# Chunk bounds in four groups of 192 queries in place of three of 256, with a new order of the work

## The chip, the cores and the metric

The kernel runs on one core of one Trainium2 chip. The metric is the time of one execution in microseconds on the device; the median of several runs is compared. One further execution was taken with the hardware profiler; all rows shown in this document come from such profiled executions.

An engine runs its own list of instructions in the order in which they were written. PE is the matmul engine (PEld its weight loads), DVE, ACT and POOL are the three element-wise engines, and SP issues DMAs; ACT and POOL issue some DMAs too.

## The reference

`q`, `k`, `v` have the shape (4, 8, 768, 64): 4 batches, 8 heads, 768 positions, 64 values each. The 768 keys are cut into 24 chunks of 32.

```python
k_min, k_max = min and max of each chunk of keys, value by value
ub = np.sum(np.maximum(q * k_min, q * k_max), axis=-1)      # an upper bound, query x chunk
ub = np.where(causal, ub, -1e9)
top_chunks = np.argsort(ub, axis=-1)[..., -6:]              # 6 best chunks of each query
scores = scale * q @ k^T, kept where the chunk is selected and the key isn't later
attn = exp(scores - max) / sum;  x = attn @ v               # 3072 tokens x 512
xn = x / rms(x) * rms_g
out = (silu(xn @ w_gate) * (xn @ w_val)) @ w_out            # 512 -> 1536 -> 512
```

## The kernel before

**The order.** The kernel first records all work as steps (`add`, line 251): each has a name, the engines that can do it, a cost, steps that it waits for, and buffers that it opens and uses. `Order.run` (line 98) then plays through time with these costs. Whenever an engine is free it takes, of the steps that are ready and whose buffers are free, the one with the lowest rank; the ranks are the numbers of `RANK` (by kind of step) and `TIMES` (by pair, half and so on). Loads also wait for a modelled DMA queue (`load=`, bytes). The instructions are emitted in the order found, so the ranks decide at build time what each engine does after what, and for steps with two engines also which does them. On the chip nothing is rearranged.

**The work.** Heads are taken in 16 pairs (four batches of four pairs). For each pair:

- `prep` loads the natural `k` and `q` (`load`, line 473; SP issues, for pair 0 half of them on ACT's queue), turns them on PE (`pk`, `pq`, line 498) into tiles with the 64 values of two heads on 128 partitions, and copies these out of PSUM (`kt`, `qt`, through `evict`, line 294 on ACT, 298 on DVE or POOL). DVE makes the chunk minima and maxima (lines 526, 524) and relu(q) (`rt`, line 568); a small subtraction gives max-min (line 542). POOL casts `kt` and `qt` to bf16 into `ke` and `qs` (for pair 0 ACT can too).
- `bounds` (line 580): ub = k_min.q + (k_max-k_min).relu(q) as fp32 matmuls of 64 rows x 32 columns. The array works as small tiles: 2 heads (row halves) x `G`=3 query groups of 256 (column quarters, so one quarter stays empty), twice (q, then relu(q)). `ub_out` copies two banks of 96x256 to SBUF, and `up_turn` (line 606) turns them back in 4 fp32 transposes, so that queries are on partitions.
- `causal` (line 616) adds the causal mask `cmf`, `top` (12 MAX8, line 631) finds the sixth best, `pick` (lines 639, 644) writes a 0/1 selection into `selq`.
- `sel_turn` (line 652) turns the selection back in 6 bf16 transposes (`st`), and `sel_out` (line 662) copies it in two instructions of 64x768 into the lower or upper half of `qs`, beside the bf16 queries. The rows of `ke` beside the keys hold the chunk pattern `e_all`, so that one score matmul does q.k and masks the chunks that aren't selected.
- `scores` (line 695): per head 6 groups of up to 4 blocks of 128x128 (in the fourth pair 2+4, first for the first half of the queries): `sc` matmuls (line 720), exp on ACT (`pt`, line 737), `av` matmuls (line 756), division (`xb`, line 772). A score matmul needs all copies of `sel_out` of its pair.

When the four pairs of a batch are done (the first half of its queries, then the second), `norm` makes the RMS norm (line 784 on) and `ffn` (line 864) the gated layer of this half: 12 times `gp` (line 884), tanh (`sg`, line 891), `tg` (line 897), `vp` (line 905), `hh` (line 913), and then `po` (line 925) with its copy `osb` and the store. The FFN of one batch and the attention of the next are interleaved by the ranks. 48 matmuls on zeros (`busy`, line 341) with the very highest rank fill PE where it has nothing else at the start; when they are used up, PE just waits.

Buffers: 3 sets of `ke`/`qs` (a pair takes the set of the pair three before it, once that one's scores have read it), 8 PSUM banks in all, with at most 3 or 4 for each use.

Of the kernel before, what the change touches and what calls it, by code (L numbers as in the profile page):

```python
# [27 lines left out]
        av=-54.4, dif=153.56, eps=344.72, exp=240.32, kC=97.58, kE=-137.82, kT=-251.02,  # L28
        kload=-3.44, kmn=111.29, kmx=140.51, max=-119.32, qC=-50.04, qE=82.16, qT=78.53,
        qload=-6.31, relu=104.93, root=78.28, sc=-65.68, sel=-319.81, selC=97.58, selT=30.75,  # L30
        sq=-238.56, tp=-62.89, tpE=19.78, ub=-202.6, ubE=-209.78, ubm=-332.23, up=-63.52,
        vload=-104.93, xb=103.6, xs=136.36,
    ),
    dict(
        av=-215.29, dif=107.84, eps=-215.03, exp=7.63, gate=-8.03, hh=-205.95, kC=167.33,
        kE=72.49, kT=-66.96, kload=51.54, kmn=-276.29, kmx=192.91, mask=-58.77, max=54.84,
        out=129.36, po=13.13, poE=7.91, qC=306.28, qE=72.26, qT=40.02, qload=32.65, relu=60.21,
        root=-87.97, sc=-65.32, sel=94.37, selC=311.72, selT=-46.08, sq=135.68, tanh=225.22,
        tg=3.41, ub=56.8, ubE=-99.19, ubm=110.82, up=42.39, val=-2.21, vload=16.42, xT=6.57,
        xb=49.3, xs=44.15,  # L40
# [161 lines left out]
def kernel(  # L202
# [26 lines left out]
    G = 3  # L229
# [83 lines left out]
    SELQ = [const.tile([P, NT, 2, D], BF16, name=f"selq{i}") for i in range(SLOTS["selq"])]  # L313
    VX = [const.tile([P, 2 * NT, D + 1], BF16, name=f"vx{i}") for i in range(SLOTS["vext"])]
    e_all = const.tile([D, S], BF16, name="e_all")
    cmf = const.tile([P, NT, 2, NCH], FP32, name="cmf")
# [27 lines left out]
    for i in range(BUSY):  # L344
# [34 lines left out]
    for i in range(NB):  # L379
        if i == 0:  # L380
            c_ke[i] = add("ke0", "", {"DVE": 1.05, "ACT": 1.4}, {"ke0": 1.0}, lambda e: (
                evict(e, KE[0][0][D:2 * D, :], e_all[:]),
                evict(e, KE[0][1][0:D, :], e_all[:])), [c_e])
        else:
            c_ke[i] = add("ke", "SP", 1.0, {"ke": 1.0}, lambda e, i=i: (
                nc.sync.dma_start(out=KE[i][0][D:2 * D, :], in_=e_all[:]),
                nc.sync.dma_start(out=KE[i][1][0:D, :], in_=e_all[:])), [c_e], load=200000)

    def make_cmf(n):
        if n == 0:  # L390
            nc.gpsimd.memset(cmf[:], 0.0)
        for g4 in (2 * n, 2 * n + 1):
            nc.gpsimd.affine_select(
                out=cmf[32 * g4:32 * (g4 + 1)], in_=cmf[32 * g4:32 * (g4 + 1)],
                compare_op=ALU.is_ge, fill=-BIGC,
                base=g4, pattern=[[4, NT], [0, 2], [-1, NCH]], channel_multiplier=0,
            )

    c_cm = add("cmf", "POOL", 1.5, -70, lambda e: make_cmf(0), [c_e])
    c_cm = add("cmf", "POOL", 1.1, -69, lambda e: make_cmf(1), [c_cm])  # L400

    def make_tri(e):
# [11 lines left out]
        load=200000)  # L414
# [14 lines left out]
    for part in range(2):  # L429
        a = add("wg", "POOL", 0.8, {f"w{part}": 1.0},  # L430
                lambda e, part=part: load_w(part, wg, moe_w_gate), load=1200000)
        b_ = add("wv", "POOL", 0.8, {f"w{part}": 1.0, "w": 1.0},
                 lambda e, part=part: load_w(part, wv, moe_w_val), load=1200000)
        c_w.append((a, b_))
    c_wo = [add("wo", "POOL", 0.8, {f"w{2 + part}": 1.0}, lambda e, part=part: load_wo(part),
                load=1200000) for part in range(2)]
# [15 lines left out]
    def load_v(c, lr):  # L452
# [7 lines left out]
        c.vload = add("v", "POOL", 1.08, rank(lr, b, "vload"), go, c_vx, opens=[c.v], load=393216)  # L460

    def prep(c, i0, nb, at, lr):
# [7 lines left out]
        for w, src in (("k", k), ("q", q)):  # L470
# [12 lines left out]
            if p == 0:  # L483
                ld = [add(w + "load", "SP", 0.55, -200 + 2 * (w == "q") + r0 / 3,
                          lambda e, load=load, r0=r0: load(e, r0=r0, rn=3), opens=[nat[w]],
                          load=3 * P * 512) for r0 in range(0, nb, 3)]
            else:
                ld = [add(w + "load", "SP", 1.1, rank(lr, b, w + "load"), load, opens=[nat[w]],
                          load=n * 512)] * 2
# [86 lines left out]
        nj = nq // P  # L576
# [411 lines left out]
```

## Time and profile before

| | us |
|---|---|
| median of 3 runs | 328.93 (328.64 to 329.02) |
| the profiled execution | 328.01 |
| its span (first to last instruction) | 326.3 |
| PE busy in the span | 314.2 (96%) |
| DVE busy | 237.8 (73%) |
| ACT busy | 201.3 (62%) |
| POOL busy | 117.4 (36%) |

In the rows below "busy, mean ns of one" stands behind a count x; a row of the chain or of the timeline begins with its start and its length in us. The time of a run is some 1.7 us above the span of its trace.

### The profile page before, as it was taken

The page shows a single profiled execution, that of the slowest core. Times are in us where ns is not written, and L with a number is a line of the kernel's source. Part 1 is how long each engine was busy: PE and PEld are TensorE (multiplying, and loading weights), DVE is VectorE, ACT ScalarE, POOL GpSimd, SP SyncE. Part 2 cuts the span into 40 slices and gives each one's busy share as a digit, 9 for nine tenths or more (in the row PEclk, how much of TensorE's full clock was granted, in tenths as well). Part 3 has the DMA queues.
Part 4 walks back from the last instruction along what each step waited for, and adds up shares of the span by engine and source line. Part 5 has one row for each costly group of instructions (what it writes and reads, how often), then busy time and mean ns, then how long its engine had stood idle before and what let it go on. Part 6 is the DMA issues. An engine that isn't in the chain of part 4 may idle for free.

```text
span 326.3 us, 7875 instructions
## 1 busy us (share of the span) xinstructions
PE 314.2 (96%) x2953; PEld 200.1 (61%) x2972; DVE 237.8 (73%) x652; ACT 201.3 (62%) x440; POOL 117.4 (36%) x176
## 2 busy tenths in 40 slices
PE   5899998999999999999999999999999999999995
PEld 2568766666776655666586776655567645666442
DVE  3578988999997589867289989587885684788200
ACT  4349999944797872564595987834399924342121
POOL 8449763644287730016062374830023120000000
PEclk9799999999999999999999999999999999999999
DMA  9999999379908998503233034510000034000123
GB/s 174 231 216 193 200 214 208 57 148 163 126 5 78 160 221 174 145 19 26 96 85 25 2 27 41 101 45 3 32 2 2 3 104 121 3 0 2 64 77 116
DMA packets 92501, 30.25 MB, mean 93 GB/s; under 512 B 85424, under 2 KB 89264, under 8 KB 92464
## 3 DMA queue, kind: packets, MB, share of 16 engines
q1 hardware_dynamic: 62352, 21.50, 29.6%
q0 software_dynamic: 28512, 7.87, 24.3%
q10 hardware_dynamic: 1600, 0.39, 0.6%
q8 instruction: 23, 0.38, 0.5%
q14 instruction: 14, 0.11, 0.1%
HBM read 28.57 MB, written 6.29 MB: 107 GB/s over the span
## 4 chain that ended last, share of the span: by engine, by line
PE 86%; ACT 5%; issue 2%; DMA 2%; DVE 2%; POOL 2%; POOLq 0%; ACTq 0%
PE vp L905 18%; PE gp L884 18%; PE po L925 18%; PE sc L720 9%; PE av L756 6%; PE ub L586 5%; PE busy L341 4%; PE pk L498 3%; PE pq L498 3%; DMA vx<-in_v_dram 2%; PE up L610 2%; ACT pt L737 1%; PE st L655 1%; ACT junk L799 1%; ACT qs L294 1%
## 5 line engine op out<-in xcount | busy, mean ns | idle before, releaser
L737 ACT ACTIVATE pt<-sc 128x512 bf16<-128x512 f32 (+3 forms) x192 | 88.4, 598 | 2.5 <-PE sc L720 2.1
L891 ACT ACTIVATE sg<-gp 128x384 bf16<-128x384 f32 x96 | 47.8, 506 | 49.0 <-PE gp L884 46.6
L905 PE MATMUL vp<-xT,wv 128*128 128x384 bf16 x384 | 75.3, 326 | 0.0
L884 PE MATMUL gp<-xT,wg 128*128 128x384 bf16 x384 | 74.7, 326 | 0.0
L897 DVE SCALAR_TENSOR_TENSOR tg<-sg,gp 128x384 bf16<-128x384 bf16 x96 | 52.0, 549 | 18.4 <-ACT sg L891 16.4
L925 PE MATMUL po<-wo,hh 128*128 128x512 bf16 x271 | 64.5, 379 | 0.9
L913 DVE TENSOR_TENSOR hh<-vp,tg 128x384 bf16<-128x384 f32 x96 | 52.3, 552 | 6.3 <-PE vp L905 4.9
L720 PE MATMUL sc<-qs,ke 128*128 128x128 bf16 (+5 forms) x419 | 53.0, 250 | 0.5 <-ACT qs L294 0.4
L884 PEld LDWEIGHTS <-wg 128*128 128x128 bf16 x384 | 36.5, 98 | 23.7 <-issue 0.4
L743 POOL TENSOR_SCALAR_AFFINE_SELECT pt<-pt 128x512 bf16<-128x512 bf16 (+1 forms) x48 | 24.9, 534 | 72.4 <-ACT pt L737 72.0
L905 PEld LDWEIGHTS <-wv 128*128 128x128 bf16 x384 | 36.5, 98 | 23.1 <-issue 0.8
L925 PEld LDWEIGHTS <-hh 128*128 128x128 bf16 x288 | 27.7, 98 | 29.0
L756 PE MATMUL av<-vx,pt 128*128 128x65 bf16 x672 | 35.1, 194 | 2.2 <-ACT pt L737 1.3
L756 PEld LDWEIGHTS <-pt 128*128 128x128 bf16 x672 | 30.0, 98 | 11.6 <-ACT pt L737 2.5
L720 PEld LDWEIGHTS <-ke 128*128 128x128 bf16 (+1 forms) x420 | 30.2, 97 | 10.2 <-issue 1.7
L296 ACT ACTIVATE osb<-po 128x512 f32<-128x512 f32 x22 | 13.3, 605 | 37.4 <-PE po L925 37.4
L298 POOL CAST qs<-qt 64x768 bf16<-64x768 f32 x31 | 28.0, 906 | 17.2 <-ACT qt L294 8.4
L298 POOL CAST ke<-kt 64x768 bf16<-64x768 f32 x31 | 25.6, 827 | 4.0 <-PE sc L720 2.0
L828 DVE SCALAR_TENSOR_TENSOR xs<-xb,ri,gains 128x512 bf16<-128x512 bf16 x24 | 18.0, 775 | 2.3 <-POOL ri L820 2.3
L772 DVE TENSOR_TENSOR xb<-av,rden 128x384 bf16<-128x384 f32 (+1 forms) x34 | 18.2, 534 | 1.2
L498 PE MATMUL pq<-ident_f,qnat 128*128 128x128 f32 x96 | 15.9, 285 | 3.2 <-issue 3.1
L631 DVE MAX8 m<-ubm 128x8 f32<-128x24 f32 x192 | 18.6, 167 | 0.1
(72 smaller groups left out, 331.4 us busy)
## 6 DMA issues: line engine op xcount, KB each, us to landing
out_dram<-osb SPq DMA_DIRECT2D x24, 256.0 KB, 2.1
qnat<-in_q_dram SPq DMA_DIRECT2D x30, 192.0 KB, 4.5
knat<-in_k_dram SPq DMA_DIRECT2D x30, 192.0 KB, 5.1
vx<-in_v_dram POOLq DMA_DIRECT2D x16, 192.0 KB, 5.7
wg<-in_moe_w_gate_dram POOLq DMA_DIRECT2D x2, 768.0 KB, 8.7
wv<-in_moe_w_val_dram POOLq DMA_DIRECT2D x2, 768.0 KB, 9.1
wo<-in_moe_w_out_dram POOLq DMA_DIRECT2D x2, 768.0 KB, 8.2
ke<-e_all SPq DMA_DIRECT2D x4, 96.0 KB, 4.8
```

The costliest lines, as they stand in the source:

```text
L298: engine[e].tensor_copy(out_, in_)
L498: nc.tensor.transpose(t[:, j * P:(j + 1) * P], nat[w].tile[:, j0 + j].rearrange("p h d -> p (h d)"), ident_f[:])
L720: nc.tensor.matmul(t[:, x:x + m, :].rearrange("p a b -> p (a b)"), ke[kk, kb * P:(kb + 1) * P], qs[kk, q0 * P:(q0 + m) * P], start=not tri ...
L737: nc.scalar.activation(out=t[:, 0:nn, :], in_=sc.tile[:, 0:nn, :], func=ACT.Exp, scale=SCALE)
L743: nc.gpsimd.affine_select(out=pt.tile[:, 0:nd, :], in_=pt.tile[:, 0:nd, :], compare_op=ALU.is_ge, fill=0.0, base=0, pattern=[[0, nd], [1, ...
L756: nc.tensor.matmul(av.tile[:, qi - i0, :], pt.tile[:, x, :], VX[c.v.slot][:, hl * NT + kb, :], start=(begin and m == 0), stop=(left[0] == ...
L884: nc.tensor.matmul(t[:], wg[:, g, hs], XT[b].tile[:, g, cols], start=(g == 0), stop=(g == NP - 1))
L891: nc.scalar.activation(out=t[:], in_=gp.tile[:], func=ACT.Tanh, scale=0.5)
L897: nc.vector.scalar_tensor_tensor(out=t[:], in0=sg.tile[:], scalar=1.0, in1=gp.tile[:], op0=ALU.add, op1=ALU.mult)
L905: nc.tensor.matmul(t[:], wv[:, g, hs], XT[b].tile[:, g, cols], start=(g == 0), stop=(g == NP - 1))
L913: nc.vector.tensor_tensor(out=t[:], in0=vp.tile[:], in1=tg.tile[:], op=ALU.mult)
L925: nc.tensor.matmul(po.tile[:], hhs[ht].tile[:, th * P:(th + 1) * P], wo[:, ht, :], start=(ht == 0), stop=(ht == NHT - 1))
```

## The change

Five things are changed.

1. `G` goes from 3 to 4: the bounds are computed in four query groups of 192 (all four column quarters). Per pair there are 16 fp32 matmuls of 192 columns in place of 12 of 256 (a trace counts two passes for each: 32 and 24). The two banks are copied out as 128x192 in place of 96x256.
2. With 4 x 32 = 128 rows the result is turned in 3 full 128x128 transposes (`NU`=3) in place of 4 of 96; the selection is turned back in 3 in place of 6, since four groups stand side by side in one transpose. The mask `cmf` is laid out anew for this and takes 8 POOL instructions at the start in place of 4.
3. The selection copies: eight of 32x192 per pair (2 heads x 4 groups), each free to go to ACT or DVE, in place of two of 64x768. As only 32 of 64 rows are written now, the other 32 of `qs` are zeroed once (3 memsets).
4. Costs and loads in the order's model: the loads of pair 0 take 0.2 in place of 0.55 each, and the bytes of loads are changed. With it, ACT issues the first two `q` loads directly after the `k` loads; before, its activation table load and the first activation stood between them.
5. All ranks are new, and so is the whole order of the instructions on every engine. In the new order the first `gp` comes when 124 score and mask matmuls (the four pairs of batch 0) have been issued; before it came after 150 (with a good part of pair 4).

```diff
-    G = 3
+    G = 4
+    NU = 3
...
+    c_qz = [add("qs0", "DVE", 0.28, -89.5 + i, lambda e, i=i: nc.vector.memset(
+        QS[i][1][CH:D, :], 0.0)) for i in range(NB)]
...
-                ld = [add(w + "load", "SP", 0.55, -200 + 2 * (w == "q") + r0 / 3,
+                ld = [add(w + "load", "SP", 0.2, -200 + 2 * (w == "q") + r0 / 3,
                           lambda e, load=load, r0=r0: load(e, r0=r0, rn=3), opens=[nat[w]],
-                          load=3 * P * 512) for r0 in range(0, nb, 3)]
+                          load=3 * P * 550) for r0 in range(0, nb, 3)]
...
         def up_turn(e):
-            t = tile_of(up, [P, G, nj, 2, CH], FP32, "up")
-            for j in range(nj):
-                for h in range(2):
-                    nc.tensor.transpose(
-                        t[:, :, j, 1 - h, :], ubs.tile[:, h, j * P:(j + 1) * P],
-                        ident_f[0:G * CH, 0:G * CH])
+            t = tile_of(up, [P, NU, G * CH], FP32, "up")
+            flat = ubs.tile[:].rearrange("p h q -> p (h q)")
+            for u in range(NU):
+                nc.tensor.transpose(t[:, u], flat[:, u * P:(u + 1) * P], ident_f[:])
...
-            t = tile_of(st, [P, nb * P], BF16, "st")
-            for j in range(nb):
+            t = tile_of(st, [P, NU * P], BF16, "st")
+            for u in range(NU):
                 nc.tensor.transpose(
-                    t[:, j * P:(j + 1) * P], SELQ[sq.slot][:, j].rearrange("p h c -> p (h c)"),
+                    t[:, u * P:(u + 1) * P], SELQ[sq.slot][:, u].rearrange("p g c -> p (g c)"),
                     ident_b[:])
...
-        for hl, rows in ((0, slice(D, P)), (1, slice(0, D))):
-            def sel_out(e, hl=hl, rows=rows):
-                evict(e, QS[c.set.slot][hl][rows, cols], st.tile[rows, :])
-
-            fin.append(add("selC", "", {"DVE": dve(n / 2), "ACT": act(n)},
-                           rank(at, b, "selC", hl, "step"), sel_out, [sT],
-                           opens=[c.set], uses=[st]))
+        for hl in range(2):
+            for g in range(G):
+                def sel_out(e, hl=hl, g=g):
+                    rows = slice((1 - hl) * D, (1 - hl) * D + CH)
+                    evict(e, QS[c.set.slot][hl][rows, g * nq:(g + 1) * nq],
+                          st.tile[g * CH:(g + 1) * CH, hl * nq:(hl + 1) * nq])
+
+                fin.append(add("selC", "", {"DVE": dve(nq / 2), "ACT": act(nq)},
+                               rank(at, b, "selC", hl, "step"), sel_out, [sT],
+                               opens=[c.set], uses=[st]))
```

Left out of the diff: the two tables of numbers, `RANK` and `TIMES`, in which every entry is replaced; the new layout of `cmf`, `ubm`, `m8` and `selq`; the changed `load=` figures.

More of the change, by code (lines that the diff above doesn't have):

```diff
@@ L386 @@
                 nc.sync.dma_start(out=KE[i][0][D:2 * D, :], in_=e_all[:]),
[L387 removed]
+                nc.sync.dma_start(out=KE[i][1][0:D, :], in_=e_all[:])), [c_e], load=180000)
     def make_cmf(n):
@@ L391, in make_cmf @@
             nc.gpsimd.memset(cmf[:], 0.0)
[L392 to L400, printed above, removed]
+        for r in (2 * n, 2 * n + 1):
+            for us, base in ((slice(0, 3, 2), r), (slice(1, 2), r + 4 if r < 2 else r - 2)):
+                x = cmf[32 * r:32 * (r + 1), us]
+                nc.gpsimd.affine_select(
+                    out=x, in_=x, compare_op=ALU.is_ge, fill=-BIGC, base=base,
+                    pattern=[[2, x.shape[1]], [6, G], [-1, NCH]], channel_multiplier=0)
+    c_cm = add("cmf", "POOL", 1.9, -70, lambda e: make_cmf(0), [c_e])
+    c_cm = add("cmf", "POOL", 1.6, -69, lambda e: make_cmf(1), [c_cm])
     def make_tri(e):
@@ L627, in top @@
                 if m8.tile is None:
-                    tile_of(m8, [P, NT, 2, 8], FP32, "m8")
-                for x in range(j, j + 3):
-                    for h in range(2):
-                        nc.vector.max(out=m8.tile[:, x, h, :], in_=ubm.tile[:, x, h, :])
+                    tile_of(m8, [P, 2 * NT, 8], FP32, "m8")
+                for x in range(2 * j, 2 * j + 6):
+                    nc.vector.max(out=m8.tile[:, x, :], in_=ubm.tile[:, x, :])
             last = add("max", "DVE", 0.52, rank(at, b, "max", j, "step"), top, [last], opens=[m8], uses=[ubm])
```

72 lines of the change are left out of this document (34 added, 38 removed), and 30 rows, old and new, of the table TIMES.

## The prediction

> **What bounds the kernel now.** I read the page first: busy shares, slices, and the chain that ended last; then the windows view, cut where the first FFN matmul starts (61.7) and near the end.
>
> ```profile
> PE 314.2 (96%) x2953; PEld 200.1 (61%) x2972; DVE 237.8 (73%) x652; ACT 201.3 (62%) x440; POOL 117.4 (36%) x176
> ...
> PE   5899998999999999999999999999999999999995
> ...
> PE 86%; ACT 5%; issue 2%; DMA 2%; DVE 2%; POOL 2%; POOLq 0%; ACTq 0%
> ```
>
> ```profile
> core 0: us, PE busy (x) PEld busy (x) DVE busy (x) ACT busy (x) POOL busy (x), PEclk, DMA share, GB/s
> 0.00:22.50 22.50, 18.09 (x126) 10.19 (x128) 11.72 (x37) 8.44 (x15) 13.79 (x30) 0.92 1.12 207
> 22.50:61.70 39.20, 36.97 (x535) 27.77 (x535) 34.53 (x126) 38.13 (x86) 22.64 (x31) 1.00 1.21 182
> 61.70:300.00 238.30, 236.86 (x2192) 151.72 (x2206) 187.94 (x484) 149.94 (x333) 81.01 (x116) 1.00 0.43 69
> ```
>
> The windows split the run in three. From 61.7 to 300 PE is busy 236.86 of 238.30 us: here time is PE work, and what DVE or ACT do beside it costs nothing as long as PE isn't kept waiting. From 22.5 to 61.7 **ACT** is the full engine (38.13 of 39.20), DVE close behind (34.53); PE looks busy, but part of that is the 48 filler matmuls. Before 22.5 no engine is full: a chain of latencies of pair 0 runs. So there are two prices: PE work after the first `gp`, and the moment of the first `gp`, which the start chain and then ACT set.
>
> **The change, part by part.** First PE work, from the chain in order of time and the timeline:
>
> ```profile
> 36.92 1.01 PE ub L586 x24
> 39.24 0.36 PE up L610 x4
> 40.41 0.34 PE st L655 x6
> 101.45 0.66 PE pk L498 x6
> ```
>
> ```profile
> 36.85 0.65 PE L586 MATMUL ub<-qt,ku 64*32 64x256 f32 x12
> 37.31 0.62 PE L586 MATMUL ub<-rt,ku 64*32 64x256 f32 x12
> ```
>
> ```profile
> L586 PE MATMUL ub<-qt,ku x6: 400/400/400, 36.9 to 36.9; 64*32 64x256 f32 x6
> ```
>
> - Bounds: six fp32 turns of 128 columns take 0.66, that is 0.11 per 128 columns, so 256 columns cost 0.22. Twelve small-tile matmuls of 256 columns take 37.31 - 36.85 = 0.46, about 2 x 0.22: six run side by side, and a pair is 4 such batches plus about 0.15 of changeover (1.01). With 192 columns a batch costs 0.16 if eight run side by side as six do: 4 x 0.16 + 0.15 = **0.80, saving 0.21 per pair**. That eight do isn't in this trace; the bounds are 0 saved (a batch costs more for more tiles) and 0.25 (a quarter of 1.01). I take 0.21, as six cost no more than one.
> - `up`: 3 x 0.11 = 0.33 for 0.36: nothing. `st`: 3 for 6, half of 0.34: **0.17 saved**.
> - Over 16 pairs 16 x 0.38 = 6.1 us of PE work; only what lies behind the first `gp` counts directly.
>
> The Trainium skill speaks against the first term: "TensorE: Matmul & The Clock Gate", section "Wait — 56ns, not 53.3ns?", says that matmuls never start closer than about 25 ns. By that rule eight starts take 0.20, so a batch costs 0.20 and not 0.16, and the time would be 1.6 us above my sum (0.16 for each of 10 pairs). The row above bears against it: six starts all lie between 36.85 and the query's end at 36.89, under 8 ns apart.
>
> In the order before, the bounds of 10 pairs, `st` of 10 and 286 score and mask matmuls stand behind the first `gp`; in the new order 10, 12 and 312. Ten score matmuls cost 0.88 (second row below), so 26 more are +2.3. Bounds -10 x 0.21 = -2.1; `st` 12 x 0.17 - 10 x 0.34 = -1.4. **Work behind the first gp: -1.2 us.**
>
> ```profile
> 105.47 1.15 PE av L756 x37
> ...
> 107.63 0.88 PE sc L720 x10
> ```
>
> Next the copies. Rows of the timeline, ACT then DVE:
>
> ```profile
> 5.53 0.87 ACT L294 ACTIVATE kt<-pk 128x384 f32<-128x384 f32 x2 [2.12 <-PE pk L498]
> 31.05 0.65 ACT L294 ACTIVATE ubs<-ub 96x256 f32<-96x256 f32 x2
> 40.84 1.62 ACT L294 ACTIVATE qs<-st 64x768 bf16<-64x768 bf16 x2
> 43.40 5.32 ACT L737 ACTIVATE pt<-sc 128x128 bf16<-128x128 f32 x12
> ```
>
> ```profile
> 47.77 0.54 DVE L298 COPY qs<-st 64x768 bf16<-64x768 bf16 x1
> 48.23 1.10 DVE L631 MAX8 m<-ubm 128x8 f32<-128x24 f32 x12
> ```
>
> On ACT two `kt` (384 columns) start 0.38 apart and two `ubs` (256) 0.27, as they overlap; by that line 192 columns cost 0.22. But a `qs` copy of 768 occupies ACT for its whole 0.81, and by its rate with a fixed part a piece of 192 costs up to 0.34. I take the middle, **0.28**; 0.22 and 0.34 are the ends. On DVE the 768 copy costs 0.46 (48.23 - 47.77); a piece costs a quarter plus an issue of at most 0.09 (MAX8: 1.10/12), 0.16 to 0.20. The new order puts 77 pieces on ACT and 51 on DVE (before 19 and 13 copies): 21.6 + 9.2 = 31 us for 15.4 + 6.0 = 21, so +10 us on two engines. Behind the first `gp` both have room (187.94 and 149.94 of 238.30), so there I cost it at nothing; without that cover it would be up to 7 us. In the ACT-bound stretch it counts.
>
> **When does the first gp come?** Rows of pair 0's chain (first the chain and PE, then ACT, then DVE):
>
> ```profile
> 5.92 3.08 issue
> 9.00 0.87 PE pq L498 x3
> ...
> 14.96 1.01 PE ub L586 x24
> ```
>
> ```profile
> 1.91 1.28 ACT L333 ACT_TABLE_LOAD   x1 [1.91 <-issue]
> ...
> 4.25 1.24 ACTq L479 DMA_DIRECT2D qnat<-in_q_dram  x2
> ...
> 23.76 3.43 ACT L737 ACTIVATE pt<-sc 128x128 bf16<-128x128 f32 x8
> ...
> 63.51 1.01 ACT L891 ACTIVATE sg<-gp 128x384 bf16<-128x384 f32 x2
> ```
>
> ```profile
> 17.43 0.46 DVE L618 TENSOR_TENSOR ubm<-up,cmf 128x288 f32<-128x288 f32 x1
> 17.80 0.94 DVE L526 TENSOR_REDUCE ku<-kt 128x24 f32<-128x768 f32 x1
> ...
> 20.66 0.46 DVE L639 SCALAR_TENSOR_TENSOR selq<-m,ubm 128x288 bf16<-128x288 f32 x1
> ```
>
> PE waits 3.08 us, until 9.00, for `q` of pair 0, whose ACT loads are issued at 4.25, behind table load and first activation. In front of these they go out at about 1.9, so `pq` can come near 6.8. From there I walked the new order by these durations: second `pq` 8.0, relu done 10.2, bounds 11.3 (pair 1's `k` turns and fillers stand ahead), mask 13.4, the selection 16.1 (no long reductions between the MAX8 now; a relu of pair 1 is), `st` 17.5 (pair 1's bounds and 14 fillers are queued ahead of it on PE; whoever is late there delays pair 0's copies), pieces until 19.1, two `kt`, first exp at **20.1** for 23.76. The ends: 21.5 (the 2.3 of the loads alone) and 18.5 (the fillers hold nothing up). POOL's four added mask instructions and ACT's two further casts (pair 0's casts, four now) fall in idle time of this stretch (8.44 and 13.79 of 22.50 are busy); without it they would cost 2 us. The three memsets stand before `kt` on an idle DVE.
>
> ```profile
> 53.37 0.63 ACT L799 ACTIVATE junk<-xb 128x512 bf16<-128x512 bf16 x1
> ...
> 59.27 0.67 ACT L294 ACTIVATE xT<-tp 128x512 bf16<-128x512 bf16 x1
> ```
>
> From the first exp to the first `sg` ACT needs 63.51 - 23.76 = 39.75 us now and is full. Counted in the new order: 10 exps less (-10 x 5.32/12 = -4.4), 4 `kt` and 1 `qt` less (-5 x 0.38 = -1.9), 5 `ubs` of 0.22 for 6 of 0.27 (-0.5), 17 pieces of 0.28 for 5 copies of 0.81 (+0.7), one square sum and two `xT` copies more (0.63 and 2 x about 0.5 by the two rows above: +1.6). Sum -4.5, so the first `sg` at 20.1 + 35.3 = 55.4, and the first `gp`, which in the new order stands right before it, at **54.6 for 61.7: -7.1 us**. With all ends the first `gp` is at 51.5 to 58.
>
> Stalls behind it: with every instruction at the mean of its row, DVE's work from `tg` 1 to 13 is 17.8 us in the new order, for 16.7 of PE's from `gp` 1 to 13 (before 18.2 for 19.9), so PE will wait: **+1.0** (0 to 3).
>
> Sum: -7.1 - 1.2 + 1.0 = -7.3 against the profiled 328.0, hence 320.7; the median lies 0.9 above that execution, so I predict **321.5** for 328.9.
>
> **The rivals.**
>
> - *The start doesn't come earlier.* POOL issues the first `gp`'s weights behind casts that wait for pair 2's scores and behind pair 4's and 5's queries; or DVE, whose 34.53 of 39.20 leave little, takes ACT's place as the bound. Rows: `wg` goes out at 37.94 now and has 24 us in hand; a load of it takes 8.7 (below). By my walk the new order issues it near 46, so it lands at 54.5, just in time. If the first `gp` stays near 61, only -1.2 and at best another -1 remain: **327**.
>
> ```profile
> 37.94 0.79 POOL L420 DMA_DIRECT2D wg<-in_moe_w_gate_dram  x1
> ```
>
> ```profile
> wg<-in_moe_w_gate_dram POOLq DMA_DIRECT2D x2, 768.0 KB, 8.7
> ```
>
> - *Slower: exps without cover.* All 12 later pairs are now computed behind the first `gp`. A pair's exps cost ACT 5.32 (the x12 above). PE needs about 3.6 for the same pair: ten score matmuls hold 16 of its 42 blocks, so 0.88 x 42/16 = 2.3, and 42 `av` at 1.15/37 are 1.3. Where FFN work doesn't fill the rest, PE waits 1.7 per pair, up to 20 us in all, plus the 7 of pieces; it decides from 8.3 us on, about five pairs uncovered, and with eight **333**. For it: long runs of `sc` and `av` in the new order between the first and the second batch's FFN. Against: from the 21st to the 25th `gp`, the densest stretch, PE has 50 us of work for ACT's 36.
> - *Eight tiles don't run side by side* (the 25 ns rule as a mechanism: a batch costs by its starts): **323**.
> - *The change doesn't do what it says:* it does, by the order of the instructions; the `q` loads do go first.
>
> **How the numbers follow.** Forecast 0.65 (318 to 325); start not earlier 0.18 (325 to 328); exps uncovered 0.10 (329 to 335); eight tiles not parallel 0.07 (323). The range takes in the ends of the first `gp` and of the stalls: 328.9 - 10.2 - 1.2 = 317.5, less 1 for the pieces in the long stretch, and 328.9 - 3.7 - 1.2 + 3 = 327: **316.5 to 327**. What a measurement can tell from no change is about 0.2% (0.7 us). Faster 0.87, same 0.04 (the edge of the first rival), slower 0.09.
>
> **What would show it.** The chain: `ub` pieces of about 0.80 and `st` of 0.17. The timeline: ACT's `qnat` issue near 1.9, `pq` near 7, first exp near 20, first `gp` near 54.6, pieces on ACT 0.28 apart. Windows: PE full from the first `gp` on. It is wrong if the first `gp` is past 58, or if PE's idle time behind it is over 4 us.

## The result and the profile after

The changed kernel takes **332.15 us** (median of 4 runs, 331.92 to 334.32) against 328.78 for the kernel before in the same series (327.8 to 329.02). The ratio is 1.013, with a 95% interval of 1.010 to 1.016: slower by about 1.3%, and 10.6 us above the 321.5 of the forecast. The profiled execution is the one of 334.32 us, with a span of 332.6 (before 326.3); the other three lie between 331.92 and 332.24.

From the page of the changed kernel: busy times, the chain by engine, and the two groups of selection pieces (busy time and mean ns of one, then the idle time just before them and what ended most of it).

```profile
PE 316.3 (95%) x3036; PEld 198.7 (60%) x3036; DVE 249.3 (75%) x698; ACT 210.4 (63%) x497; POOL 118.5 (36%) x176
...
PE 73%; ACT 15%; DVE 8%; issue 3%; ACTq 0%; DVEq 0%
...
L295 ACT ACTIVATE qs<-st 32x192 bf16<-32x192 bf16 x77 | 24.7, 321 | 16.1 <-DVE qs L299 12.3
...
L299 DVE COPY qs<-st 32x192 bf16<-32x192 bf16 x51 | 12.8, 252 | 12.2 <-ACT qs L295 10.6
```

And the 64x768 copies of the kernel before, from its groups kept apart by shape:

```profile
L294 ACT ACTIVATE qs<-st 64x768 bf16<-64x768 bf16 x19 | 15.3, 806 | 1.9 <-PE st L655 1.7
L298 DVE COPY qs<-st 64x768 bf16<-64x768 bf16 x13 | 7.2, 552 | 5.0 <-ACT qs L294 4.5 <-PE st L655 0.4
```

PE's share of the chain fell from 86% to 73%, that of ACT and DVE rose from 7% to 23%. The copies were 22.5 us of engine time and are 37.5. Beside that stands a cost that no busy share shows: ACT waits 12.3 us for a piece on DVE to end, DVE 10.6 for one on ACT (before 4.5 in all).

The windows of the changed kernel, cut as before:

```profile
core 0: us, PE busy (x) PEld busy (x) DVE busy (x) ACT busy (x) POOL busy (x), PEclk, DMA share, GB/s
0.00:22.50 22.50, 21.08 (x171) 12.71 (x172) 16.55 (x58) 13.40 (x27) 14.72 (x36) 1.00 1.19 200
22.50:61.70 39.20, 34.58 (x495) 24.16 (x494) 34.04 (x101) 33.90 (x88) 21.80 (x27) 0.96 1.17 186
61.70:300.00 238.30, 231.99 (x2221) 147.05 (x2220) 187.32 (x520) 154.60 (x367) 81.96 (x114) 1.00 0.44 70
```

In the long stretch PE is busy 231.99 us where it was 236.86, with DVE no busier than before (187.32) and ACT 4.7 us busier (154.60). From 22.5 to 61.7 ACT is no longer full: 33.90 of 39.20.

The chain of the changed kernel and ACT's timeline show the start:

```profile
6.13 0.64 PE pq L501 x3
...
11.04 0.81 PE ub L588 x32
...
12.87 0.33 PE up L612 x3
...
17.46 0.17 PE st L651 x3
...
58.01 2.40 PE gp L883 x8
```

```profile
1.91 1.06 ACTq L482 DMA_DIRECT2D qnat<-in_q_dram  x2
...
21.06 5.36 ACT L736 ACTIVATE pt<-sc 128x128 bf16<-128x128 f32 x12
...
26.19 2.66 ACT L295 ACTIVATE qs<-st 32x192 bf16<-32x192 bf16 x8
...
59.17 0.49 ACT L890 ACTIVATE sg<-gp 128x384 bf16<-128x384 f32 x1 [1.21 <-PE gp L883]
```

The first `gp` comes at 58.0, which is 3.7 earlier than before. But from there to the end of the span it is 332.6 - 58.0 = 274.6, for 326.3 - 61.7 = 264.6 before: 10.0 longer, though the instructions that PE has there are those of the forecast, 1.2 us less work than before. A small part of it is the clock. Two more windows of the changed kernel:

```profile
54.00:58.00 4.00, 2.29 (x47) 1.39 (x32) 4.00 (x9) 3.96 (x12) 3.15 (x3) 1.00 1.11 218
...
58.40:61.80 3.40, 3.40 (x12) 1.55 (x11) 1.79 (x5) 0.98 (x2) 0.52 (x1) 0.50 1.04 144
```

Just before the first `gp` PE is busy 2.29 of 4.00 us, and then its granted clock is 0.50 for 3.4 us, which is worth up to 1.7 us. The other three executions, with a mean granted clock of 0.997 to 1.000 for 0.993 here, are some 2 us shorter. So about 8 of the 10.0 us remain. One place where they go, from the timeline of all engines:

```profile
183.83 0.32 ACT L295 ACTIVATE qs<-st 32x192 bf16<-32x192 bf16 x1 [0.54 <-PE st L651]
...
184.79 0.25 DVE L299 COPY qs<-st 32x192 bf16<-32x192 bf16 x1
...
185.07 0.32 ACT L295 ACTIVATE qs<-st 32x192 bf16<-32x192 bf16 x1 [0.92 <-DVE qs L299]
185.43 0.26 DVE L299 COPY qs<-st 32x192 bf16<-32x192 bf16 x1 [0.39 <-ACT qs L295]
185.72 0.32 ACT L295 ACTIVATE qs<-st 32x192 bf16<-32x192 bf16 x1 [0.33 <-DVE qs L299]
186.07 0.25 DVE L299 COPY qs<-st 32x192 bf16<-32x192 bf16 x1 [0.39 <-ACT qs L295]
...
186.36 0.66 ACT L295 ACTIVATE qs<-st 32x192 bf16<-32x192 bf16 x2 [0.32 <-DVE qs L299]
...
187.06 0.81 PE L883 MATMUL gp<-xT,wg 128*128 128x384 bf16 x4 [1.22 <-ACT qs L295]
```

One pair's eight pieces run from 183.83 to 187.02, strictly one after the other: all read the one PSUM bank of `st`. But for the second, whose engine was still at other work, a piece on the other engine starts 0.03 to 0.04 after the one before has ended. The releasers in brackets are read from semaphores, so it is waits in the program that keep the two engines apart; no run here lets both read the bank at once. While one works the other waits with its whole queue. The next `gp` gets its bank when the last piece has ended, and PE stands for 1.22 us.

### The profile page after: what moved, and what is told of

Its sections match the earlier page's. It is cut to its first block, busy times and chain, and to the rows that moved or that the text cites. A ratio compares the mean times of both kernels' runs of the same rounds, so it can differ in the third digit from the quotient of the medians.

```text
span 332.6 us, 8116 instructions
## 1 busy us (share of the span) xinstructions
PE 316.3 (95%) x3036; PEld 198.7 (60%) x3036; DVE 249.3 (75%) x698; ACT 210.4 (63%) x497; POOL 118.5 (36%) x176
## 4 chain that ended last, share of the span: by engine, by line
PE 73%; ACT 15%; DVE 8%; issue 3%; ACTq 0%; DVEq 0%
PE po L924 17%; PE gp L883 15%; PE vp L904 15%; PE sc L719 8%; ACT pt L736 6%; PE av L755 5%; ACT qs L295 4%; PE busy L342 4%; PE ub L588 3%; PE pq L501 3%; PE pk L501 3%; DVE qs L299 2%; DVE tg L896 2%; DVE hh L912 2%; ACT junk L798 1%
## 5 line engine op out<-in xcount | busy, mean ns | idle before, releaser
L736 ACT ACTIVATE pt<-sc 128x512 bf16<-128x512 f32 (+3 forms) x192 | 89.4, 601 | 2.5 <-PE sc L719 2.3
L890 ACT ACTIVATE sg<-gp 128x384 bf16<-128x384 f32 x96 | 47.0, 496 | 56.4 <-PE gp L883 54.8
L883 PE MATMUL gp<-xT,wg 128*128 128x384 bf16 x384 | 77.7, 329 | 4.0 <-ACT qs L295 2.9
L904 PE MATMUL vp<-xT,wv 128*128 128x384 bf16 x384 | 78.1, 328 | 0.3 <-ACT qs L295 0.3
L924 PE MATMUL po<-wo,hh 128*128 128x512 bf16 x288 | 69.7, 379 | 0.0
L912 DVE TENSOR_TENSOR hh<-vp,tg 128x384 bf16<-128x384 f32 x96 | 52.5, 553 | 13.4 <-PE vp L904 10.1
L719 PE MATMUL sc<-qs,ke 128*128 128x128 bf16 (+5 forms) x420 | 55.4, 251 | 3.5 <-ACT qs L295 1.1
L883 PEld LDWEIGHTS <-wg 128*128 128x128 bf16 x384 | 37.2, 99 | 30.1 <-issue 5.6
L742 POOL TENSOR_SCALAR_AFFINE_SELECT pt<-pt 128x512 bf16<-128x512 bf16 (+1 forms) x48 | 25.9, 555 | 76.0 <-ACT pt L736 75.7
L295 ACT ACTIVATE qs<-st 32x192 bf16<-32x192 bf16 x77 | 24.7, 321 | 16.1 <-DVE qs L299 12.3
L299 POOL CAST ke<-kt 64x768 bf16<-64x768 f32 x30 | 24.9, 831 | 24.1 <-ACT kt L295 19.1
L299 DVE COPY qs<-st 32x192 bf16<-32x192 bf16 x51 | 12.8, 252 | 12.2 <-ACT qs L295 10.6
```

Of the source, the lines that this page charges most:

```text
L295: nc.scalar.activation(out=out_, in_=in_, func=ACT.Copy)
L299: engine[e].tensor_copy(out_, in_)
L719: nc.tensor.matmul(t[:, x:x + m, :].rearrange("p a b -> p (a b)"), ke[kk, kb * P:(kb + 1) * P], qs[kk, q0 * P:(q0 + m) * P], start=not tri ...
L736: nc.scalar.activation(out=t[:, 0:nn, :], in_=sc.tile[:, 0:nn, :], func=ACT.Exp, scale=SCALE)
L742: nc.gpsimd.affine_select(out=pt.tile[:, 0:nd, :], in_=pt.tile[:, 0:nd, :], compare_op=ALU.is_ge, fill=0.0, base=0, pattern=[[0, nd], [1, ...
L883: nc.tensor.matmul(t[:], wg[:, g, hs], XT[b].tile[:, g, cols], start=(g == 0), stop=(g == NP - 1))
```

## The experiments

Three theories stood at first. **H**: the handoffs between ACT and DVE at the bank cost. **O**: the new order starves PE by itself. **W**: the pieces need too much engine time. Then **S** (one serial chain per pair) and **W2** (the time for which pieces and their turns hold the queues). All diffs are against the changed kernel unless another is named; each ratio is to the kernel before.

**1. all_dve**

```python
-        s.emit(s.eng)
+        s.emit("DVE" if s.name == "selC" else s.eng)
```

> The order of the changed kernel is kept; only all eight selection copies of a pair go to DVE (in the changed kernel 77 of 128 are on ACT). Theory H (handoffs): the eight copies read one PSUM bank, so ACT and DVE take turns with a wait at each change of engine, and the matmuls that need the bank, or that need ACT and DVE work queued behind the waiting copies, come late. Without the turns a pair's copies take about 8 x 0.17 to 0.25 = 1.4 to 2.0 us, PE loses 4 to 7 us behind the first gp in place of 14.5, and the time is 322 to 326 us. Theory O (order): the new order of the steps itself starves PE, whoever copies: 330 us or more. Theory W (work): the copies just need too much engine time: DVE gets some 8 us more work and the time rises above 332.

338.69 us (ratio 1.035, 1.029 to 1.041): 6.5 slower than the changed kernel, without a single handoff. H alone falls. Its group:

```profile
L299 DVE COPY qs<-st 32x192 bf16<-32x192 bf16 x128 | 32.2, 252 | 3.1 <-PE st L651 1.1
```

DVE, the fuller engine, carries 32.2 us of pieces, and that costs more than 60 us of pieces and turns on two engines.

**2. alternate**

```python
+        if s.name == "selC":
+            seen[s.bufs[-1]] = n = seen.get(s.bufs[-1], -1) + 1
+            e = ("ACT", "DVE")[n % 2]
```

> The order of the changed kernel is kept; the eight copies of a pair alternate ACT, DVE, ACT and so on: 112 changes of engine within pairs in place of about 52 waits between the two in the changed kernel. H: each change costs some 0.35 us of a pair's copy chain, which gets 1 to 1.5 us longer, and the time rises by 3 to 8 us, to 335 to 340. O: 332 as before, since the order is the same. W: ACT has 13 copies less, 64 on each, so the time falls a little, 330 to 332.

338.78 (1.034, 1.029 to 1.038). Every piece waits for the other engine: a pair takes 3.07 us from first piece to last (2.72 in the changed kernel, 1.62 before, means over 16 pairs).

**3. new_bounds_old_order**: the kernel before, in its exact order, with the new bounds, turns and pieces.

```python
-                evict(e, QS[c.set.slot][hl][rows, cols], st.tile[rows, :])
...
+                for g in range(G):
+                    evict(e, QS[c.set.slot][hl][rows, g * nq:(g + 1) * nq],
+                          st.tile[g * CH:(g + 1) * CH, hl * nq:(hl + 1) * nq])
```

> Four groups of 192, three turns each way and eight copies, but in the very order of the kernel before (its ranks, costs and loads; the four copies of a head are one step on one engine, the three memsets go with others). H: at most one change of engine in a pair, as before; PE work falls by 6.1 us, the copies of a head take 1.0 to 1.3 in place of 0.5 to 0.8 us, so the start stage is 1 to 2 us later: 324 to 328 us. O: the same forecast, since the old order is the good one: below 328. W: above 329, as the copies cost more than PE saves.

335.32 (1.025, 1.020 to 1.030): the new bounds and pieces lose in the old order too, at the start (first `gp` at 65.8) and behind it (268.1).

**4. old_bounds_new_order**: the changed kernel's order, with the old bounds, six turns and two 64x768 copies.

```python
+                    if g == 0:
+                        rows = slice((1 - hl) * D, (2 - hl) * D)
+                        evict(e, QS[c.set.slot][hl][rows, cols], st.tile[rows, :])
```

> The order of the changed kernel, but three groups of 256, four and six turns, and two copies of 64x768 (made where the first of a head's four copies stood, on its engine; the other three steps issue nothing). H: the turns at the bank go; PE work rises by 6.1 us and the lost time behind the first gp falls from 14.5 to 4 to 6: 326 to 330 us. O: the stalls stay and the PE work comes back: 336 to 339.

326.09 (0.993, 0.990 to 0.996): faster than both. O falls: the first `gp` comes at 55.7, and from 61.7 to 300 PE is busy 237.94 of 238.30 us, so this order doesn't starve it. What the order gains beside the early loads, q_first (12) tells.

**5. no_copies**

```python
-                    evict(e, QS[c.set.slot][hl][rows, g * nq:(g + 1) * nq],
-                          st.tile[g * CH:(g + 1) * CH, hl * nq:(hl + 1) * nq])
+                    return
```

> The changed kernel without any of the 128 selection copies (the selection rows of the query set are zeroed once at the start, so the choice of chunks is left out); bounds, turns, selection and the order of all other steps stay. Theory S (the copies of a pair form one serial chain behind one PSUM bank, and that chain is what costs): the time falls to 319 to 322, which is old_bounds_new_order's 326.1 less the 6.1 of TensorE work, and the loss behind the first gp falls from 14.5 to 3 to 5. Rival B (the new bounds and their turns starve TensorE themselves, copies or not): 327 or more, loss over 9.

318.27 (0.971, 0.964 to 0.977). The 128 pieces cost **13.9 us** of time. Of the span they cost 15.8: the first `gp` comes at 53.8 (4.2 earlier), and from there to the end it is 316.8 - 53.8 = 263.0 (11.6 less). Its windows:

```profile
22.50:61.70 39.20, 36.52 (x536) 27.50 (x536) 35.91 (x101) 32.22 (x79) 23.85 (x28) 1.00 1.22 205
61.70:300.00 238.30, 236.65 (x2247) 151.71 (x2267) 186.45 (x490) 139.26 (x314) 79.06 (x111) 1.00 0.42 68
```

PE is full again in the long stretch (236.65), with all the new bounds and turns in place. The loss against the kernel before belongs to the pieces. (This trace has no stretch of half clock behind the first `gp`, so some 10 of the 11.6 are theirs.)

**6. one_head**

```python
+                    if hl == 0:
                         evict(e, QS[c.set.slot][hl][rows, g * nq:(g + 1) * nq],
```

> The changed kernel with the four pieces of one head left out in every pair (its selection rows are zeroed once at the start, so the choice of chunks is left out for that head): 64 pieces in place of 128, order otherwise kept. Between no copies (318.3) and all (332.2). If every piece costs the same: 325. Theory S, a chain that has to be longer than the slack behind it (before's chain of 1.5 to 1.6 cost little): 319 to 322, less than half of the loss of 13.9.

320.58 (0.977, 0.974 to 0.981). The first half of the pieces costs 2.3 us, the second 11.6. Behind the first `gp` (55.8) it is 262.8, no more than with none: there is cover, and it ends between half and all.

**7. same_quadrant**

```python
-                          st.tile[g * CH:(g + 1) * CH, hl * nq:(hl + 1) * nq])
+                          st.tile[0:CH, hl * nq:(hl + 1) * nq])
```

> The changed kernel with every piece read from partitions 0 to 31 of the turned selection in place of the group's own 32, so that consecutive pieces start on the same partitions (the content of the selection is wrong, amount and form of the work the same). Theory S with holding (a piece waits for the piece before to end because its first partition differs): ACT pieces come 0.22 apart in place of 0.33, DVE 0.17 in place of 0.255, the chain of a pair shortens from 2.7 to about 2.0, and the time falls to 327 to 330. If the pieces are spaced by something else (size, bank): spacing and time stay, 331 to 333.

328.02 (1.001, 0.999 to 1.004), 4.1 less than the changed kernel. ACT's timeline has the same eight pieces that took 2.66 at 26.19:

```profile
25.50 1.94 ACT L295 ACTIVATE qs<-st 32x192 bf16<-32x192 bf16 x8
```

Less the last piece's 0.32 and over seven steps that is 0.23 apart in place of 0.33: pieces overlap if they start on the same partitions, and don't if the start changes. One step of the seven is still 0.34: there the head changes, and with it the partitions that are written. On DVE the median distance falls from 0.265 to 0.175. The Trainium skill states such a rule ("VectorE: DVE Perf Modes", section "Two Vector instructions with no wait between them": an instruction is held until the earlier ones have finished if its input or output starts in another group of 32 partitions than the last one that read, or wrote, that memory). The trace agrees for DVE, and ACT, of which the page does not speak there, does the same.

**8 and 9. two_banks, one_bank**

```python
+        sts = [st, Buf("ps")]
...
+                          sts[hl].tile[g * CH:(g + 1) * CH, hl * nq:(hl + 1) * nq])
...
+            for g in range(4):
+                cs[g].emit("ACT")
+                cs[4 + g].emit("DVE")
```

(one_bank: `sts = [st, st]`.)

> The selection turned into two PSUM banks (four transposes in place of three, 0.055 each, so 0.9 more of TensorE work in all); ACT copies the four pieces of head 0 from one, DVE the four of head 1 from the other, all eight at the place of the pair's first piece in the queues. In 15 of the 16 pairs; in one there is no free bank, it stays at one. Theory S (one bank makes the pieces take turns): ACT and DVE work at the same time, the chain of a pair takes 1.3 to 1.6, and the time is 323 to 327. Rival W (the engines' time for the copies is what costs, 0.33 and 0.255 each, wherever they are read): no better than one_bank, 330 or more.

> The same as two_banks (same queues, four transposes, ACT head 0, DVE head 1, all at the place of the pair's first piece), but both heads read from one PSUM bank. Theory S: the pieces take turns, chain 2.4 to 3.1 per pair, time 330 to 336, that is 5 to 10 above two_banks. Rival W: within 2 of two_banks.

two_banks 332.79 (1.014, 1.006 to 1.021), one_bank 346.17 (1.053, 1.045 to 1.060), above the 330 to 336 that S gave it. Their groups, two_banks first:

```profile
L295 ACT ACTIVATE qs<-st 32x192 bf16<-32x192 bf16 x64 | 20.5, 320 | 4.8 <-PE st L653 2.9 <-DVE qs L299 0.9
L299 DVE COPY qs<-st 32x192 bf16<-32x192 bf16 x64 | 16.0, 250 | 3.7 <-ACT qs L295 1.8 <-PE st L653 1.2
```

```profile
L295 ACT ACTIVATE qs<-st 32x192 bf16<-32x192 bf16 x64 | 20.5, 320 | 22.1 <-DVE qs L299 16.2 <-PE st L653 5.5
L299 DVE COPY qs<-st 32x192 bf16<-32x192 bf16 x64 | 16.0, 250 | 23.2 <-ACT qs L295 22.9 <-PE pk L501 0.2
```

The engine time is the same to a tenth; only the turns differ: 2.7 us of waiting against 39.1, and 13.4 us of time. So 36 us of turns cost 13.4 us of time, about as much per us as the pieces themselves (see the table). But two_banks did not reach the 323 to 327 that S gave it: a chain of 1.5 us per pair, all at one place in both queues, still loses 8 us behind the first `gp` (58.6, 270.9); its fourth turn on PE is under 1 of them. And one_bank's chain is no longer than the changed kernel's (2.58 us per pair against 2.72), yet it is 14 us slower: there all pieces stand at one place in both queues, so both engines are held for the whole chain. S alone does not do.

**10. scratch_copies**

```python
-                    evict(e, QS[c.set.slot][hl][rows, g * nq:(g + 1) * nq],
+                    evict(e, SCR[e][rows, g * nq:(g + 1) * nq],
```

> The changed kernel with all 128 pieces read from the same bank on the same engines and at the same places, but written to a tile that nobody reads (the query set's selection rows are zeroed once, so the choice of chunks is left out): scores no longer wait for the last piece. If the loss is the scores' direct wait for the chain: 318 to 321. If it is that the pieces' turns hold up what stands behind them in the queues of ACT and DVE (exponentials, evictions, sums): 328 to 332.

332.64 (1.015, 1.011 to 1.020): as slow as the changed kernel, with no score that reads what the pieces write. The loss is not the scores' wait for the selection.

**11. sbuf_copies**

```python
-                          st.tile[g * CH:(g + 1) * CH, hl * nq:(hl + 1) * nq])
+                          FLAT[g * CH:(g + 1) * CH, hl * nq:(hl + 1) * nq])
```

> The changed kernel with all 128 pieces at the same places on the same engines, written to the query set as before, but read from a constant tile of SBUF (the choice of chunks is left out): no PSUM bank in which the engines take turns, and no wait for the turned selection. Theory S (taking turns at the bank costs): 319 to 323. Rival W (the pieces' own time on the engines costs): 328 or more.

328.44 (1.000, 0.997 to 1.002), so 3.7 less than the changed kernel and 10.2 more than with no copies.

```profile
L295 ACT ACTIVATE qs<-flat 32x192 bf16<-32x192 f32 x77 | 27.7, 360 | 1.2
L299 DVE CAST qs<-flat 32x192 bf16<-32x192 f32 x51 | 17.8, 350 | 0.9
```

No turns are left, but 45.5 us of work (a piece from this fp32 tile takes longer: 0.36 and 0.35). By this run W is the larger part and S the smaller. But with the bank two more things are gone: the wait for the turned selection, and the hold on the bank for which a `gp` waited.

**12. q_first**: the kernel before, with the first q loads ahead of ACT's first activation and nothing else.

```python
+    late = next(s for s in done if s.name == "first")
+    done.remove(late)
+    done.insert(1 + max(i for i, s in enumerate(done) if s.name == "qload" and s.keys.get("", 0) < -150), late)
```

> The kernel before with one thing of the change alone: the first two q loads are issued ahead of ACT's first activation, the order otherwise kept. My start term says that the first q turns come 1.9 to 2.2 earlier and the first exponential up to 3.6 earlier with all that was moved; with the loads alone the first exponential should come 1.5 to 2.2 earlier, the first gp likewise, and the time falls by 1 to 2. Rival (the order behind it was made for the late start, something else ends last): the first gp moves by under 0.5 and the time by under 0.5.

**323.88** (0.987, 0.984 to 0.990), the fastest kernel of this study that leaves nothing out. Rows of ACT and of PE:

```profile
20.11 3.43 ACT L737 ACTIVATE pt<-sc 128x128 bf16<-128x128 f32 x8
```

```profile
57.61 0.81 PE L884 MATMUL gp<-xT,wg 128*128 128x384 bf16 x4
```

First exp 3.65 earlier than before (23.76), first `gp` 4.1 (61.69), and the time 4.4: more than the 1 to 2 expected. Behind the first `gp` nothing changes (322.2 - 57.6 = 264.6, as before). The chains of the start, before and then q_first:

```profile
5.92 3.08 issue
9.00 0.87 PE pq L498 x3
9.88 1.28 PE busy L341 x3
11.15 0.64 PE pq L498 x3
```

```profile
6.56 0.64 PE pq L498 x3
7.20 0.76 PE busy L341 x3
7.96 0.33 PE pq L498 x3
```

The first turn of `q` comes 2.4 earlier, as the loads explain. The rest is the clock: in the kernel before the granted clock is 0.50 from 8.5 to 11.9, right behind PE's idle 3.08 us, and the two turns with the fillers between them take 1.1 us longer in sum; in q_first PE has no such hole, and its granted clock up to 22.5 is 1.00 (before 0.92). The hole doesn't cost clock in every execution: single executions of the kernel before with a mean granted clock of 0.999 or more took 325.15 to 327.21 (seven of them, median 325.77), so against these q_first gains 1.9, which is within what was expected.

The whole new order with the old copies (run 4) takes 326.09, that is 2.2 more than q_first. Its first `gp` comes 1.9 earlier, but behind it the span is 4.3 longer: 26 more score matmuls and two more pairs' `st` (together some 3), and a stretch of half clock from 56.3 to 59.7 (up to 1.7). Beside the early loads the new order brings nothing.

**13. old_bounds_twice**: old_bounds_new_order with each copy done twice.

```python
                         evict(e, QS[c.set.slot][hl][rows, cols], st.tile[rows, :])
+                        evict(e, QS[c.set.slot][hl][rows, cols], st.tile[rows, :])
```

> old_bounds_new_order (326.1) with each of its two 64x768 copies per pair done twice, one right after the other to the same place: the queues of ACT and DVE are held for 46 in place of 23, bounds and turns as in the kernel before. W2: what is above some 25 to 30 costs 0.5 to 0.8 per us, so 333 to 341. If the loss of the changed kernel belongs to its small pieces or its bounds: 326 to 329.

344.81 (1.052, 1.048 to 1.057): 23 us more of copies cost 18.7 us of time, in a kernel with neither small pieces nor new bounds. W2 holds in kind, but its price was too low: at 0.8 per us the time is above the 333 to 341 that it gave.

**14 and 15. dma_pieces, pool_sbuf** (in the last 12 pairs)

```python
+                        if hl == 0 and g == 0:
+                            evict(e[0], flat[:], st.tile[:])
+                        nc.sync.dma_start(out=QS[c.set.slot][hl][rows, g * nq:(g + 1) * nq],
+                                          in_=flat[g * CH:(g + 1) * CH, hl * nq:(hl + 1) * nq])
```

(pool_sbuf: `nc.gpsimd.tensor_copy` in place of the DMA.)

> The changed kernel; in the last 12 pairs the turned selection leaves PSUM in one 128x384 copy (at the place and on the engine of the pair's first piece), and eight DMAs on SP's queue take its pieces to the query set; the first four pairs keep the eight pieces. ACT and DVE lose about 2.35 of piece time and 1.8 of turns per pair and get one copy of about 0.4. Theory W2 (what costs is the time for which the pieces and their turns hold the queues of ACT and DVE, once it is above some 25 to 30 for the whole kernel): first gp about 58 as in the changed kernel, behind it 263 to 265 as without copies, 321.5 to 325 in all. Rival (the scores need the selection soon, so a transfer of 2 or more behind the copy starves them): 330 or more.

> The same as dma_pieces, but the eight pieces go from SBUF to the query set on GpSimd (about 0.4 each by its 64x768 cast of 0.96, so 3 per pair). W2: 322 to 327; if GpSimd's own work (its casts of q) is held up by it: 328 or more.

342.58 (1.046, 1.040 to 1.051) and 333.37 (1.016, 1.011 to 1.022). What PE waits for from 53 on, first dma_pieces, then pool_sbuf (us in all, times, longest):

```profile
PE sc L727 <- DMA qs<-ss: 8.8, 11, 2.7
PE gp L891 <- DMA xT<-xs: 3.3, 1, 3.3
```

```profile
PE av L763 <- POOL pt L750: 6.9, 5, 2.7
```

No `gp` waits for a copy any more in either, as W2 says, but its times are missed by 18 and 6 us, and the rivals named beside it are right: a transfer lands 1.8 us after its issue (median), now the scores wait for it; and the pieces on POOL delay its masking of `pt`, on which `av` waits.

**16. best_dma**: q_first, with new bounds, and DMAs as in 14.

```python
+                    if isinstance(e, tuple):
+                        nc.sync.dma_start(
+                            out=QS[c.set.slot][hl][rows, g * nq:(g + 1) * nq],
+                            in_=SS[p % 4][g * CH:(g + 1) * CH, hl * nq:(hl + 1) * nq])
```

> Put together from what the runs gave: the order of the kernel before with the first q loads ahead (323.9), the new bounds, turns and selection, eight pieces in the first four pairs and one copy with eight DMAs in the other twelve. W2: 323.9 less 3 to 5 of TensorE work behind the first gp, plus up to 4 for the pieces of the first four pairs: 319 to 325.

358.94 (1.095, 1.088 to 1.102) for the 319 to 325 expected: the wait for the transfers again, now on SP too, which stands in order before each of them (DMA `qs<-ss` is 8% and SP's queue 4% of its chain). The clock adds to it: the mean granted clock of the profiled execution is 0.957 (0.978 in dma_pieces), and 4.3% of its 358.8 us are up to 15 us.

**Together.** "Held" is the busy time of the pieces or copies on ACT and DVE plus the idle time that the other engine's piece ended, from group rows as shown. "Half clock" is the time behind the first `gp`, but for the last 2 us of the span, in which the granted clock is 0.50; up to half of it is lost. Only runs in the new order are listed; the two with old bounds have some 4 us more PE work behind the first `gp` (10 x 0.20 of `ub`, 12 x 0.17 of `st`).

| kernel | time | first gp | from there to the end | half clock | held |
|---|---|---|---|---|---|
| no_copies | 318.3 | 53.8 | 263.0 | 0 | 0 |
| one_head | 320.6 | 55.8 | 262.8 | 0 | 30 |
| old_bounds_new_order | 326.1 | 55.7 | 268.9 | 3.4 | 25 |
| sbuf_copies | 328.4 | 56.7 | 270.5 | 3.4 | 46 |
| same_quadrant | 328.0 | 56.5 | 271.0 | 3.1 | 54 |
| two_banks | 332.8 | 58.6 | 270.9 | 0 | 39 |
| scratch_copies | 332.6 | 57.8 | 273.1 | 0 | 61 |
| changed kernel | 332.2 | 58.0 | 274.6 | 3.4 | 60 |
| alternate | 338.8 | 58.4 | 278.6 | 3.4 | 72 |
| one_bank | 346.2 | 61.4 | 280.2 | 0 | 76 |
| old_bounds_twice | 344.8 | 60.5 | 283.2 | 6.8 | 52 |

If half of the half clock and the extra work are taken off, old_bounds_new_order comes to 263.2 in the fourth column, as good as with no copies, and the changed kernel to 272.9, like scratch_copies. So some 25 to 30 us are free behind the first `gp`, and what goes beyond costs about 0.3 to 0.4 per us, more where it comes in one block (0.9 in two_banks, about 0.6 with the doubled copies of 0.8 us). These are prices read off a few rows, not a law. all_dve is outside this: 32 us, all on the fuller engine, cost 13.7 behind the first `gp`.

## Why the prediction was wrong

**The step that failed** is the price of the selection copies: "Behind the first `gp` both have room (187.94 and 149.94 of 238.30), so there I cost it at nothing; without that cover it would be up to 7 us", and "+10 us on two engines" before it. Three things were wrong in it. The miss adds up: the first `gp` came 3.4 us later than forecast, the rest of the span was 10.2 longer, and the median lies 2.2 below the profiled execution in place of 0.9 above it, so 3.4 + 10.2 - 3.1 = 10.5 of the 10.6.

- *The size.* A piece on ACT takes its whole 0.32 and the next starts 0.33 after it; I took 0.28, and 0.34 as the end. On DVE it is 0.25, above my bound of 0.20. Together 37.5 us for 22.5 is +15, not +10. (The 22.5 were 21 in my sum, which took the old copy on DVE at 0.46; its mean is 0.55.)
- *The turns.* I counted no wait between the pieces of a pair. They are one serial chain at one bank, and the waits of ACT and DVE for each other rose from 4.5 to 22.9 us. one_bank against two_banks prices such waits: 36 us of them, 13.4 us of time.
- *The cover.* 50 us free on DVE and 88 on ACT are a mean over 238 us. Half the pieces cost nothing behind the first `gp`, all of them 11.6 (some 10 without the stretch of half clock), so even my "up to 7 us" was too small. What seems to count is how long PE can go on when ACT or DVE stops for a moment; no run measures that by itself.

**Stalls behind it, +1.0 (0 to 3).** From the first `gp` to the end the forecast was -1.2 of work and +1.0 of stalls; measured were +10.0 in the profiled execution, of which up to 1.7 are half clock. The sign that I had named, over 4 us of PE idle time behind the first `gp`, is there: 6.3 us from 61.7 to 300. The work is as counted. The stalls weren't: I had compared DVE's and PE's sums for 13 tiles, and a sum doesn't see an engine that waits.

**The start.** Nearly all of the walk came out: issue of `qnat` 1.91 (1.9), first `pq` 6.13 in the chain (6.8), bounds 11.0 (11.3), `st` 17.5 (17.5). The pieces were to end at 19.1, and the first exp to come at 20.1; it came at 21.06, since the eight pieces, one after the other, took 2.6 in place of 1.6 and ended at 20.3. From there to the first `sg` I gave 35.3 and it took 38.1. I had let ACT stay the full engine; it is busy 33.90 of 39.20 and waits for DVE's pieces. So the first `gp` came 3.7 earlier and not 7.1. The pieces are what is missing: without them it comes at 53.8, where I gave 54.6 with them. That the early loads alone bring as much is shown by q_first (4.1); I had tied the gain to all that was moved, and had not seen that the hole in the profiled kernel before had cost clock as well as time.

**PE's work.** Right: the bounds of a pair take 0.81 (0.80 forecast), `st` 0.17 for 0.34, and `up` 0.33. The rival of eight tiles that don't run side by side, which would have given 0.95, falls. Of the first bounds only these start between 10.9 and 11.03 (the first at 10.97):

```profile
L588 PE MATMUL ub<-qt,ku x8: 347/347/347, 11.0 to 11.0; 64*32 64x192 f32 x8
```

All eight start within 0.06 us, so under 9 ns apart, where that rival needed 25.

**The rivals.** The slower one named 333, near the result, but by exps without cover, with the pieces as an addition. old_bounds_new_order has the same exps in the same places, takes 326.1 and keeps PE full from 61.7 to 300: exps were not it, the addition was. That 333 lies near the result is luck. "The start doesn't come earlier" was half true, for a reason that it did not name.

**What stays open.** How the 13.9 us that the pieces cost divide between the pieces' own time and their turns: sbuf_copies leaves 10.2 with slower pieces and no turns, same_quadrant takes 4.1 away by overlap alone, one_bank shows turns to cost as much as work; the shares don't add up to one sum, since each run also shifts what stands behind in the queues. Whether two engines could read different partitions of one bank at the same time was not tried. A layout that keeps the 0.21 per pair without small pieces was not found.

## What to carry to other kernels

An engine that is busy 63% or 79% of a stretch is not cover for any amount of more work: ask how long the bound engine can run on when the other stops, and price a split copy by its full serial time, turns included. Pieces that read one PSUM bank were one chain here, on one engine or two; four pieces, each a quarter of its columns, cost ACT 1.33 us here (4 x 0.33) where the whole took 0.81. To tell what an added step costs, leave it out, halve it and double it: here the first two, and the doubled old copies, showed at once that there is a threshold. And look at the granted clock before two times are compared: in the profiled kernel before, a hole in PE's work cost clock behind it as well.

## What the runs showed of the hardware

- Copies of 32x192 on one engine overlapped only if they started on the same partitions as the one before: 0.23 apart against 0.33 on ACT, 0.175 against 0.265 on DVE.
- A change of engine at a bank cost only 0.03 to 0.04 us (ACT's piece of 185.07 ends at 185.39, DVE's starts at 185.43); the wait is the other's whole piece.
- 32 fp32 matmuls of 64 rows x 32 columns over 192 queries took 0.81 us, eight side by side.
- SBUF to SBUF transfers of 12 KB landed 1.8 us after their issue (median), and PE waited up to 2.7 us for one.
- PE's granted clock was 0.50 for 3.4 us behind a stretch in which PE stood or half stood: from 8.5 in the kernel before (PE busy 0.01 us from 5.9 to 9.0), from 58.4 in the changed kernel (2.29 of 4.00). Three fillers took 1.28 us there in place of 0.76.
